# New entries in a list scheduler's table of times: changes of TensorE's form, scores, weighted values, early experts, and the delay of other engines' results

## The chip, the cores and the metric

One core of a Trainium2 chip runs the whole program. The metric is device time in microseconds of one execution; the kernel before takes 797.88 us (median of three runs). Its engines each work through a list of instructions of their own, in order: TensorE (matrix products and transposes; PE in the profile), VectorE (DVE), ScalarE (ACT), GpSimd (POOL), and SyncE (SP), which issues the transfers. Where one needs another's result it waits for it, and everything behind it on that engine waits too.

## The reference, cut to what matters

```python
scores = scale * np.matmul(q, k.transpose(0, 1, 3, 2))        # 2 batches, 8 heads, 576 x 576
x = (psi_rel / psi_i)[..., None]                              # from log distances of positions
bias = np.maximum(x @ w1 + b1, 0.0) @ w2                      # a network of 32 hidden units, for 8 heads
scores = scores + bias.transpose(2, 0, 1)[None, :, :, :]
attn = softmax(scores); x = np.matmul(attn, v)                # 1152 tokens x 512
for e in range(4):                                            # four experts, dense
    out += p[:, e:e + 1] * (np.maximum(x @ moe_w1[e], 0.0) @ moe_w2[e])
h = out @ w_in; g = h * np.cos(h); return g @ w_out           # 512 -> 2048 -> 512
```

## The kernel before, in words

The program is written as a graph of some 3750 steps. Each step names its engine, how long it is thought to take, what it reads and writes, and a function that emits its instructions. `Graph.order` plays the graph through on a clock of its own and so decides in which order every engine gets its instructions, which buffer a tile takes, and, for steps that two or three engines can do (`alts`), which engine does them. A step becomes ready when its inputs are done by that clock (plus `LAG` of the engine that made them) and a buffer is free; of the ready ones the one that was written down first is taken. The built program then has these orders fixed; the clock is not in it. So a number in the table of times changes no instruction, but may change every order.

TensorE runs in three forms: column tiles for the bias networks (L507, mode "columns"), row tiles for the scores (L700, mode "rows"), and the whole array for the rest. The table adds `SWITCH` to a step that changes the form.

The stages, by TensorE's work:
- The bias networks, 36 steps of 16 rows each (L507). Each needs masks that VectorE makes (L482) and ScalarE (L484, L486), and leaves two or three banks that VectorE combines (L515, L522) before SyncE writes them to memory.
- The first set of attention, the first 64 rows of all heads, in plain fp32: scores L667, transposes L652, values L676. It yields the first 128 tokens (`x0`).
- Early experts (`fill`): 7 halves of experts on these 128 tokens alone, first layer L1028 and second layer L1036 in fp32. They are written down after all else of attention and go wherever TensorE has nothing better.
- The second set, 512 rows of each head, in pairs of heads with every fp32 operand split into a high and a low fp32r half. One scoring product (`qk`, L700, 12 matmuls) serves two heads and 128 rows; then VectorE takes the row's extreme (L622), ScalarE the exponential (L625), VectorE the reciprocal in two small steps (L629, L631), GpSimd, VectorE or ScalarE scale (L635), TensorE transposes (L652), ScalarE and VectorE split into halves (L558, L560; tails L711, L713), TensorE makes the values (L720, 18 matmuls for a pair), ScalarE and VectorE add their halves (L723, L725). There are 32 scoring products. Two banks of scores exist, both taken by one product.
- The experts on all tokens (`run_ff`, `block_products`; first layer L773 and L913, second L782), their first layers split by L978 and L979, the weighted sums by L990 (the first for a tile) and L993. Weights are split by ScalarE or GpSimd (L548, L547) and VectorE or GpSimd (L549); L732 is the low half of a finished block of tokens.
- The last two layers with the cosine, on the same lines.

## Time and profile before

| what | us |
|---|---|
| median of three runs (795.89 to 800.22) | 797.88 |
| the profiled execution | 794.95 |
| its span, first to last instruction | 793.1 |
| TensorE busy in it | 776.9 |
| VectorE busy in it | 675.4 |
| ScalarE busy in it | 451.7 |
| GpSimd busy in it | 161.8 |

The granted clock of TensorE is 1.0 over the whole span. Busy time counts an instruction from its start to its modelled end, and successive instructions overlap a little; so for what a group costs I read from its start to the start of what follows it. A row of the timeline gives start, busy time, engine, line, what is written from what, and how many instructions; a bracket says how long the engine was idle before it and who released it. A matmul in plain fp32 stands as two records. Rows with "p1x" or "fx" are buffers that take over the place of earlier ones.

### The profile page before, as it was taken

How to read it: one execution, taken by the hardware profiler on the slowest of the kernel's cores; microseconds unless marked ns; L12 is line 12 of the kernel's file. 1: busy time of each engine (PE TensorE's matmuls, PEld its weight loads, DVE VectorE, ACT ScalarE, POOL GpSimd, SP SyncE). 2: the span in 40 equal slices, each digit the busy share in tenths (PEclk: the TensorE clock that was granted, in tenths of full speed). 3: DMA queues.
4: the chain of work that ended last, by engine and by line, in shares of the span. 5: the costliest groups of instructions: out<-in, count | busy, mean ns of one | idle time of the engine just before them, and what ended most of it. 6: DMA issues, size and time to landing. Idle time of an engine off the chain costs nothing.

```text
span 793.1 us, 15013 instructions
## 1 busy us (share of the span) xinstructions
PE 776.9 (98%) x5122; PEld 645.4 (81%) x5122; DVE 675.4 (85%) x1581; ACT 451.7 (57%) x956; POOL 161.8 (20%) x212
## 2 busy tenths in 40 slices
PE   7899999999999999999999999999999999999998
PEld 5575667888788878888888888888889889998997
DVE  8969998888889899578997989798879939999575
ACT  6667647787987752344563636272535637665352
POOL 0110055767985820135000000000000000000000
PEclk9999999999999999999999999999999999999999
DMA  6978989988755421645554453543453296769012
GB/s 216 293 257 254 287 305 285 274 265 249 234 161 172 133 81 41 194 163 185 176 199 147 133 199 119 193 152 125 129 184 107 91 337 208 248 218 305 25 43 79
DMA packets 98988, 148.08 MB, mean 187 GB/s; under 512 B 13280, under 2 KB 46688, under 8 KB 98912
## 3 DMA queue, kind: packets, MB, share of 16 engines
q1 hardware_dynamic: 98912, 147.13, 57.6%
q8 instruction: 40, 0.66, 0.3%
q14 instruction: 36, 0.29, 0.1%
HBM read 110.68 MB, written 36.41 MB: 185 GB/s over the span
## 4 chain that ended last, share of the span: by engine, by line
PE 89%; DVE 5%; DMA 2%; issue 1%; ACT 1%; SPq 1%; POOL 0%; DVEq 0%; ACTq 0%
PE p1x L782 20%; PE p L782 15%; PE p1x L913 10%; PE p1x L773 9%; PE p L913 7%; PE p L773 5%; PE p L507 4%; PE p L652 3%; PE p L1036 3%; PE p L720 3%; PE p L700 3%; PE p L1028 3%; PE p L676 1%; DVE bs L482 1%; DVE es L522 1%
## 5 line engine op out<-in xcount | busy, mean ns | idle before, releaser
L782 PE MATMUL p1x<-wx,hs 128*128 128x512 f32 (+1 forms) x708 | 166.7, 389 | 1.7 <-DVE hs L979 1.7
L782 PEld LDWEIGHTS p1x<-wx,hs 128*128 128x128 f32 x708 | 131.5, 188 | 28.9 <-DVE hs L979 2.3
L782 PE MATMUL p<-wx,hs 128*128 128x512 f32 (+1 forms) x516 | 122.9, 389 | 0.1
L782 PEld LDWEIGHTS p<-wx,hs 128*128 128x128 f32 x516 | 95.4, 188 | 19.7 <-DVE hs L560 0.3
L635 POOL TENSOR_SCALAR es<-es,stats 128x576 f32<-128x576 f32 (+2 forms) x104 | 63.1, 622 | 82.8 <-ACT bs L486 30.1
L773 PE MATMUL p1x<-xh,wx 128*128 128x384 f32 (+2 forms) x248 | 69.9, 355 | 0.0
L625 ACT ACTIVATE es<-es,stats 128x576 f32<-128x576 f32 x72 | 55.4, 771 | 15.4 <-DVE stats L622 5.7
L507 PE MATMUL p<-bs,wpc 128*32 128x288 bf16 (+3 forms) x1152 | 53.4, 321 | 5.9 <-DVE es L522 3.1
L622 DVE CUSTOM_DVE_ANT_0 es<-p,es 128x576 f32<-128x576 f32 x72 | 53.0, 751 | 4.5 <-PE p L700 2.1
L548 ACT ACTIVATE wx<-fs 128x512 fp32r<-128x512 f32 (+1 forms) x80 | 45.0, 582 | 19.8 <-DMA fs<-in_mw 10.0
L507 PEld LDWEIGHTS <-wpc 128*32 128x32 bf16 x1152 | 30.4, 96 | 27.5 <-issue 16.8
L773 PE MATMUL p<-xh,wx 128*128 128x384 f32 (+2 forms) x168 | 48.4, 353 | 0.6 <-DVE stats L629 0.6
L773 PEld LDWEIGHTS p1x<-xh,wx 128*128 128x128 f32 x248 | 45.4, 188 | 4.2
L482 DVE TENSOR_SCALAR bs<-cst,cneg 128x576 bf16<-128x576 f32 (+3 forms) x108 | 46.8, 472 | 0.0
L913 PE MATMUL p1x<-xh,wx 128*128 128x512 f32 (+1 forms) x144 | 45.8, 366 | 0.0
L560 DVE TENSOR_TENSOR hs<-p,hs 128x512 fp32r<-128x512 f32 x61 | 41.0, 685 | 3.4 <-ACT hs L558 2.7
L773 PE MATMUL p1x<-xl,wx 128*128 128x384 f32 (+2 forms) x124 | 43.9, 354 | 0.0
L549 POOL TENSOR_TENSOR wx<-fs,wx 128x512 fp32r<-128x512 f32 (+1 forms) x38 | 41.7, 1120 | 2.5 <-ACT wx L548 2.1
L652 PE MATMUL p<-ident,es 128*128 128x128 f32 x276 | 41.9, 278 | 0.3 <-POOL es L635 0.3
L913 PE MATMUL p1x<-tx,wx 128*128 128x512 f32 (+1 forms) x180 | 41.6, 367 | 0.0
L558 ACT ACTIVATE hs<-p 128x512 fp32r<-128x512 f32 x61 | 35.7, 594 | 9.4 <-PE p L652 8.8
L549 DVE TENSOR_TENSOR wx<-fs,wx 128x512 fp32r<-128x512 f32 (+1 forms) x56 | 36.7, 675 | 5.0 <-ACT wx L548 4.9
(237 smaller groups left out, 1686.8 us busy)
## 6 DMA issues: line engine op xcount, KB each, us to landing
fs<-in_mw SPq DMA_DIRECT2D x119, 256.0 KB, 4.1
wx<-winhl SPq DMA_DIRECT2D x32, 256.0 KB, 5.5
wx<-wouthl SPq DMA_DIRECT2D x32, 256.0 KB, 5.2
es<-biasD SPq DMA_DIRECT2D x24, 288.0 KB, 4.6
winhl<-fs SPq DMA_DIRECT2D x23, 256.0 KB, 2.8
wouthl<-fs SPq DMA_DIRECT2D x23, 256.0 KB, 3.2
fs<-in_win SPq DMA_DIRECT2D x22, 256.0 KB, 3.6
fs<-in_wout SPq DMA_DIRECT2D x20, 256.0 KB, 3.8
```

The lines of the kernel that those rows point to most:

```text
L482: e.tensor_scalar(out=mask(t), in0=tab[:, w0:w0 + W], scalar1=cneg[:, u:u + 1], scalar2=None, op0=ALU.is_ge)
L507: nc.tensor.matmul(out=pv(a)[32 * t:32 * t + 32], lhsT=wpc[:, i, 32 * kk:32 * kk + 32], rhs=mask(t, m * a, m), start=(i == 0), stop=(i == ...
L548: act = ("ACT", t_act(n, 0, 1), lambda: nc.scalar.activation(out=hv(), in_=fv(), func=AF.Copy))
L549: low = lambda e: e.tensor_tensor(out=lv(), in0=fv(), in1=hv().bitcast(F32), op=ALU.subtract)
L560: G.step("DVE", t_dve(n), lambda: nc.vector.tensor_tensor(out=dst(AL), in0=src(), in1=dst(AH).bitcast(F32), op=ALU.subtract), rd=[ps_, (AH ...
L622: G.step("DVE", t_dve(S) + 10, lambda: nc.vector.tensor_tensor_reduce(out=f3(bt.tile[:, :S]), in0=sp.tile[:, :, 0:288], in1=f3(bt.tile[:, ...
L625: exp_all.append(G.step("ACT", t_act(S, 1, 1) + 67, lambda: nc.scalar.activation(out=e.tile[:, :S], in_=bt.tile[:, :S], func=AF.Exp, scale ...
L635: nrm = lambda g: g.tensor_scalar(out=dst(), in0=src(), scalar1=rs, scalar2=1.0, op0=ALU.mult, op1=ALU.mult)
L652: nc.tensor.transpose(tp.tile[:, 128 * kt:128 * kt + 128], e.tile[:, 128 * kt:128 * kt + 128], ident)
L773: nc.tensor.matmul(out=z.tile[:, 0:n], lhsT=w[dt][2][wi]()[:, 128 * ft:128 * ft + 128], rhs=x[:, dt, p0:p0 + n], start=(dt == 0 and i == 0 ...
L782: nc.tensor.matmul(out=y.tile[:, 0:m], lhsT=hx, rhs=w[ft][2][wi]()[:, c0:c0 + m], start=(ft == 0 and i == 0), stop=(ft == nf - 1 and i == 2))
L913: nc.tensor.matmul(out=z.tile[:, 0:n], lhsT=x()[:, 128 * t:128 * t + 128], rhs=y(), start=(start and d == 0 and i == 0), stop=(d == 1 and ...
```

## The change

The table gets new numbers: what a change of form costs, per form, less the time that TensorE has been idle; how late results of other engines reach TensorE (`TO_PE`, used in place of `LAG` where the reader is TensorE); and the durations of the scoring product, the exponential, the two small steps, the values and the early experts' first layer. No step is added or taken away. The two lines that come in shift later line numbers by one or two.

```diff
-    SWITCH, STAY = 91.0, 0
+    TO_PE = {"ACT": 250.0, "DVE": 245.0, "POOL": 175.0, "DMA": 207.0}
+    SWITCH, STAY = {"columns": 93.0, "rows": 196.0, "": 196.0}, 0
...
-                    s.dur, mode = s.dur + self.SWITCH, s.mode
+                    s.dur, mode = s.dur + max(0.0, self.SWITCH[s.mode] - (now - eng_free[e])), s.mode
...
+                tp = s.end + s.lat + self.TO_PE.get(e, 0.0)
...
-                    k.rdy = max(k.rdy, s.end if same else t)
+                    k.rdy = max(k.rdy, s.end if same else tp if k.eng == "PE" else t)
...
-T_QK = 800.0
+T_QK = 770.0
...
-        exp_all.append(G.step("ACT", t_act(S, 1, 1) + 67, lambda: nc.scalar.activation(
+        exp_all.append(G.step("ACT", t_act(S, 1, 1) + 104, lambda: nc.scalar.activation(
...
-        G.step("DVE", 73, lambda: nc.vector.tensor_scalar(
+        G.step("DVE", 86, lambda: nc.vector.tensor_scalar(
...
-        G.step("DVE", 73, lambda: nc.vector.reciprocal(
+        G.step("DVE", 80, lambda: nc.vector.reciprocal(
...
-                G.step("PE", 9 * t_mm(256), av, rd=[V, AH, AL, AT], wr=[(bank, "av")])
+                G.step("PE", 9 * t_mm(256) + 33, av, rd=[V, AH, AL, AT], wr=[(bank, "av")])
...
-            ends["l1"] = G.step("PE", 4 * 218, l1, rd=w1s + [fix("x0")], wr=[z])
+            ends["l1"] = G.step("PE", 4 * 223, l1, rd=w1s + [fix("x0")], wr=[z])
```

It changes the orders from the first microseconds on. Three places follow; `p` are banks of PSUM, `es` the tiles of scores and bias, `bs` the masks.

First place, VectorE in the first set of attention. Before, the seventh and the eighth pass over scores (L622) and what stands between:

```order
L622 ISA es_135,stats<-p_162,es_135 128x576
L622 ISA stats 128x1
L684 COPY x_82<-p_157 64x64
L629 TENSOR_SCALAR stats<-stats 128x1
L631 RECIPROCAL stats<-stats 128x1
L565 COPY es_134<-p_156 64x128
L622 ISA es_133,stats<-p_162,es_133 128x576
```

And now, around the sixth and the seventh pass (L624):

```order
L517 SCALAR_TENSOR_TENSOR es_134<-p_154,cst 128x512
L484 TENSOR_SCALAR bs_152<-cst,cneg 128x384
L524 SCALAR_TENSOR_TENSOR es_134<-p_157,es_134 128x512
L624 ISA es_138,stats<-p_162,es_138 128x576
L624 ISA stats 128x1
L484 TENSOR_SCALAR bs_149<-cst,cneg 128x384 x3
L460 RECIPROCAL psum_p<-psum_p 128x9
L517 SCALAR_TENSOR_TENSOR es_138<-p_154,cst 128x384
L631 TENSOR_SCALAR stats<-stats 128x1
L624 ISA es_132,stats<-p_161,es_132 128x576
```

Pieces of the bias (L517 and L524, which were L515 and L522, and the masks L484, which were L482) now stand between the passes over scores, where before only the pieces of the first set stood.

Second place, VectorE at the beginning of the second set, around the first two passes over scores. Before:

```order
L522 SCALAR_TENSOR_TENSOR es_138<-p_157,es_138 128x288
L622 ISA es_133,stats<-p_162,es_133 128x576
L622 ISA stats 128x1
L622 ISA es_134,stats<-p_161,es_134 128x576
L622 ISA stats 128x1
L522 SCALAR_TENSOR_TENSOR es_139<-p_156,es_139 128x288
L629 TENSOR_SCALAR stats<-stats 128x1
L522 SCALAR_TENSOR_TENSOR es_139<-p_155,es_139 128x288
```

Now:

```order
L524 SCALAR_TENSOR_TENSOR es_142<-p_154,es_142 128x288
L624 ISA es_139,stats<-p_162,es_139 128x576
L624 ISA stats 128x1
L624 ISA es_131,stats<-p_161,es_131 128x576
L624 ISA stats 128x1
L551 TENSOR_TENSOR ks_128<-fs_104,ks_127 128x512
L631 TENSOR_SCALAR stats<-stats 128x1
L624 ISA es_140,stats<-p_161,es_140 128x576
```

The last bias pieces now all stand ahead of the first pass; on TensorE the first two scoring products, which had 24 bias matmuls (L507) between them, now stand one behind the other.

Third place, TensorE at the hand-over to the experts, right behind the last value product. Before, the end of a second-layer group (L782) and the first-layer group behind it (L773):

```order
L782 MATMUL p_157<-wx_3194,hs_94 128x512
L782 MATMUL p_157<-wx_3195,hs_94 128x512
L773 MATMUL p1x_4020<-xh,wx_3091 128x512
L773 MATMUL p1x_4020<-xl,wx_3091 128x512
L773 MATMUL p1x_4020<-xh,wx_3091 128x512
L773 MATMUL p1x_4020<-xh,wx_3070 128x512
```

Now:

```order
L784 MATMUL p_155<-wx_3325,hs_89 128x512
L784 MATMUL p_155<-wx_3324,hs_89 128x512
L775 MATMUL p_155<-xh,wx_3904 128x384
L775 MATMUL p_155<-xl,wx_3904 128x384
L775 MATMUL p_155<-xh,wx_3905 128x384
L775 MATMUL p_155<-xh,wx_3264 128x384
```

Before, the first-layer group wrote another bank than the group ahead of it; now it writes the same one, p_155. Between the scoring products themselves there are now far fewer expert products (L775, L784) and more early ones (L1030, L1038).

## Rows read from the trace of the kernel before

**Rows 1.** The page's first part: busy us, share of the span, instructions.
```profile
PE 776.9 (98%) x5122; PEld 645.4 (81%) x5122; DVE 675.4 (85%) x1581; ACT 451.7 (57%) x956; POOL 161.8 (20%) x212
```

**Rows 2.** Busy us of each engine in five stretches (start:end, length, engines, clock, DMA).
```profile
core 0: us, PE busy (x) PEld busy (x) DVE busy (x) ACT busy (x) POOL busy (x), PEclk, DMA share, GB/s
...
40.00:60.00 20.00, 20.00 (x201) 14.52 (x193) 13.59 (x42) 12.56 (x32) 2.98 (x4) 1.00 0.80 261
...
100.00:115.00 15.00, 14.31 (x272) 9.39 (x270) 14.06 (x30) 5.66 (x11) 7.58 (x8) 1.00 0.84 285
115.00:263.00 148.00, 144.82 (x1132) 120.65 (x1132) 128.68 (x380) 119.34 (x278) 110.08 (x156) 1.00 0.75 229
263.00:300.00 37.00, 35.22 (x198) 30.88 (x198) 34.42 (x61) 21.96 (x47) 16.39 (x19) 1.00 0.39 114
...
500.00:550.00 50.00, 50.00 (x223) 41.40 (x222) 44.78 (x100) 22.32 (x47) 0.00 (x0) 1.00 0.45 146
```

**Rows 3.** TensorE's waits: line, for whom, us in total, times, longest.
```profile
PE p L507 <- DVE es L522: 3.1, 3, 1.7
PE p L720 <- DVE ht L713: 2.1, 2, 1.8
PE p1x L782 <- DVE hs L979: 1.7, 1, 1.7
```

**Rows 4.** Timeline of TensorE around the first two scoring products.
```profile
112.34 1.06 PE L700 MATMUL p<-ks,ks 64*128 64x288 f32 x12
113.33 0.92 PE L507 MATMUL p<-bs,wpc 128*32 128x288 bf16 x24
114.94 1.06 PE L700 MATMUL p<-ks,ks 64*128 64x288 f32 x12 [0.69 <-DVE stats L622]
```

**Rows 5.** VectorE in the first set (timeline), and the last bias pieces (groups by shape).
```profile
45.97 0.22 DVE L684 COPY x<-p 64x64 f32<-64x64 f32 x1 [0.54 <-PE p L676]
...
L522 DVE SCALAR_TENSOR_TENSOR es<-p,es 128x288 f32<-128x288 f32 x16 | 6.8, 449 | 0.1
```

**Rows 6.** Timeline of TensorE in the bias stage, with early experts.
```profile
62.76 2.94 PE L1028 MATMUL p<-x,fs 128*128 128x128 f32 x24
65.63 2.29 PE L507 MATMUL p<-bs,wpc 128*32 128x384 bf16 x48
...
70.38 1.98 PE L1036 MATMUL p<-fs,fs 128*128 128x512 f32 x4
72.29 2.46 PE L507 MATMUL p<-bs,wpc 128*32 128x448 bf16 x48
```

**Rows 7.** The chain that ended last, in order of time: start, us, what.
```profile
329.81 10.88 PE p1x L782 x48
```

**Rows 8.** VectorE's groups by shape: busy us, mean ns of one, idle before.
```profile
L622 DVE CUSTOM_DVE_ANT_0 es<-p,es 128x576 f32<-128x576 f32 x72 | 53.0, 751 | 4.5 <-PE p L700 2.1 <-PE p L667 1.7
L560 DVE TENSOR_TENSOR hs<-p,hs 128x512 fp32r<-128x512 f32 x61 | 41.0, 685 | 3.4 <-ACT hs L558 2.7
L713 DVE TENSOR_TENSOR ht<-p,ht 64x256 fp32r<-64x256 f32 x30 | 12.7, 422 | 0.5
L631 DVE RECIPROCAL stats<-stats 128x1 f32<-128x1 f32 x72 | 11.2, 159 | 1.3
```

**Rows 9.** Timeline at the hand-over: VectorE, then GpSimd.
```profile
281.56 2.39 DVE L549 TENSOR_TENSOR wx<-fs,wx 128x512 fp32r<-128x512 f32 x2
283.88 1.77 DVE L732 TENSOR_TENSOR xl<-fx,xh 128x512 fp32r<-128x512 f32 x1
...
286.16 1.28 DVE L549 TENSOR_TENSOR wx<-fs,wx 128x512 fp32r<-128x512 f32 x2
...
280.99 1.81 POOL L549 TENSOR_TENSOR wx<-fs,wx 128x512 fp32r<-128x512 f32 x1 [0.78 <-ACT wx L548]
283.56 1.53 POOL L549 TENSOR_TENSOR wx<-fs,wx 128x512 fp32r<-128x512 f32 x1 [0.76 <-ACT wx L548]
```

**Rows 10.** VectorE's first weighted sum of an expert's tile, by shape.
```profile
L990 DVE TENSOR_SCALAR fs<-p1x,prob 128x512 f32<-128x512 f32 x2 | 1.5, 752 | 2.2 <-PE p1x L782 1.4 <-issue 0.8
```

More of the change, by code (lines that the diff above doesn't have):

```diff
@@ L624, in unit @@
             op0=ALU.add, op1=ALU.min, accum_out=stats[:, 0, c:c + 1]), rd=[sp, bt], wr=[bt, (st, "m")])
-        exp_all.append(G.step("ACT", t_act(S, 1, 1) + 67, lambda: nc.scalar.activation(
+        exp_all.append(G.step("ACT", t_act(S, 1, 1) + 104, lambda: nc.scalar.activation(
             out=e.tile[:, :S], in_=bt.tile[:, :S], func=AF.Exp, scale=-1.0, bias=stats[:, 0, c:c + 1],
             accum_out=stats[:, 1, c:c + 1]), rd=[bt, (st, "m")], wr=[e, (st, "s")], after=trn_all[-AHEAD:1 - AHEAD]))
-        G.step("DVE", 73, lambda: nc.vector.tensor_scalar(
+        G.step("DVE", 86, lambda: nc.vector.tensor_scalar(
             out=stats[:, 2, c:c + 1], in0=stats[:, 1, c:c + 1], scalar1=1e-9, scalar2=None, op0=ALU.add), rd=[(st, "s")], wr=[(st, "t")])
-        G.step("DVE", 73, lambda: nc.vector.reciprocal(out=stats[:, 3, c:c + 1], in_=stats[:, 2, c:c + 1]), rd=[(st, "t")], wr=[(st, "r")])
+        G.step("DVE", 80, lambda: nc.vector.reciprocal(out=stats[:, 3, c:c + 1], in_=stats[:, 2, c:c + 1]), rd=[(st, "t")], wr=[(st, "r")])
         rs = stats[:, 3, c:c + 1]
```

## Prediction, made before the changed kernel ran

> **What bounds the kernel now.** I began with the page's first part: TensorE is busy for 776.9 us of the span of 793.1 [rows 1]. So an order of instructions can give back at most the 16.2 us in which TensorE stood idle, and some of that lies before the first operand has landed and after the last product, where no order reaches it. Then I cut the span into stages [rows 2]. From 300 us on nothing is to be had: TensorE is busy for all of 500 to 550, and the same products are left to do. The idle time sits in three places: the start (the bias networks), the scoring stage from 115 to 263 us, where TensorE works 144.82 of 148 us and so loses 3.2, and the hand-over to the experts from 263 to 300, where it loses 1.8. The waits name the releasers, and they are all on VectorE [rows 3]: 3.1 us in three waits of the bias products for L522, 2.1 in two waits of the value products (L720) for the low half of a probability tile (L713), 1.7 in one wait at the hand-over. VectorE is therefore the second thing to watch: the change has to serve it better, or it does nothing.
>
> **What the change removes.** No arithmetic goes or comes. In the order of TensorE I count 105 changes between its three forms (column tiles for the bias, row tiles for the scores, whole array) before and 103 after. A change costs some 0.2 us by the scoring products: twelve of them take 0.99 us from their start to the next start, against 0.77 that the table now holds for them [rows 4]. Two fewer, and one more folded into a wait: **-0.3 us**.
>
> **The start, up to the second scoring product.** TensorE's order is the same for the first 32 us. In the first set of heads the trace has VectorE idle for 6.4 of the 20 us from 40 to 60 [rows 2]; it waits for products of early scores and of early values, again and again for about half a microsecond, as in the first of [rows 5]. The new order puts bias pieces there (first place shown above). In exchange it takes 16 early-expert products of the first kind and 4 of the second out of the bias stage and puts them among the scores. Their price: twelve of the first kind take 2.87 us up to the next start, so 0.22 each after about 0.2 for the form; two of the second kind take 1.91, so 0.86 each [rows 6]. That is 16 x 0.22 + 4 x 0.86 = 7.0 us of TensorE work that comes later, and not less work. With the form change saved, TensorE would reach its second scoring product 7.3 us sooner than the 114.94 us of [rows 4], at 107.6. Can VectorE follow? Before that product TensorE needs the first two passes over scores (L622). In the old order two of the last bias pieces (L522) stand behind these passes, in the new order none does (second place): 2 x 0.449 [rows 5], so 0.9 us more VectorE work in front of them. Filling the whole hole of 6.4 and doing 0.9 more leads to 114.94 - 6.4 + 0.9 = 109.4 us; filling it and also the idle 0.9 of 100 to 115 [rows 2] leads to 108.5. TensorE arrives 0.9 to 1.8 us before it is let go. The two scoring products also stand back to back now, without the 24 bias products that filled 0.9 us between them [rows 4]; the wait for L622, 0.69 there, grows by as much, but this is the same wait, since TensorE was early anyway. So this stretch costs **+1.3 us**, between -1.0 (TensorE's own idle of 0.7 between 100 and 115 goes as well) and +4.0 (only half of the hole is filled).
>
> **The scoring stage.** The new order takes 90 expert products (L773, L782) out of it and puts the 7.0 us above in. At 0.227 us each (48 of them in 10.88 us, [rows 7]) that is 20.4 - 7.0 = 13.4 us less TensorE work, done later without loss, for those products fill TensorE wherever they stand. What changes the span is only the idle time. Two waits for L713 make up 2.1 of the 3.2 us [rows 3]. The new table lets results of VectorE reach TensorE 245 ns after their end instead of 165, counts the form changes at 196 instead of 91, and so no longer places a value product where it arrives a little early. I take 2.1 us back, **-2.1**. Bounds: -3.2 if all the idle time goes, and as much the other way, +3.2, because VectorE becomes tighter. Per scoring product it has two passes L622 (751 ns), two L560 (685), L713 and L725 (422, the same width) and four small ones (159): 4.35 us by [rows 8], some 4.0 where one starts before the other has ended. 31 of them are 124 us, without the splits and the early experts' sums. The stage shrinks from 148 to about 148 - 13.4 - 2.1 = 132.5. VectorE is busy for 128.68 us of it now, 87% [rows 2], the experts' work included, and would be at about 94%.
>
> **The hand-over.** The wait of 1.7 us goes: it came because two splits took 2.39 us and the low half of the last block (L732) 1.77, where the two splits right after it took 1.28 [rows 9]; GpSimd was running its own splits at 280.99 and 283.56. In the new order L732 is never on VectorE. A new wait takes its place: the last value product is followed by two second-layer groups, and the first-layer product after them writes the bank that the second of these has just filled (third place). The bank must be scaled out first by L990, 0.75 us [rows 10], and the two signals around it add, by the table, about 0.5. What is queued behind it are TensorE's own 60 first-layer products, and nothing else that is ready. 1.2 - 1.7 = **-0.5 us**, between -1.7 (another engine's delay lets the bank be free) and +1.5 (L990 itself is late by a slow split).
>
> **The rest** is TensorE without a gap before and after; moved pieces of the weight conversion have more than enough time there. 0, within 0.5.
>
> Sum: -0.3 + 1.3 - 2.1 - 0.5 = -1.6 us on the profiled execution: span 791.5, its time 794.95 - 1.6 = 793.35. The median of the three runs shown, 797.88, lies 2.9 above the profiled run; the timed kernel is compared with that, so I predict 797.88 - 1.6 = 796.3 us.
>
> **Rivals.** *VectorE becomes the bound of the scoring stage (slower).* For it: 94% by the sum above, and a VectorE instruction that meets a GpSimd one is stretched: 2.39 against 1.28 us for two splits, and 1.77 for L732, in [rows 9]. The new order gives VectorE 9 more splits of 512 columns, 3 of them among the scores. It decides from the point where VectorE's 8.5 us of slack in the stage are gone. Each stretched instruction costs about 0.55 us, so 15 of them use it up; with 24 stretched ones TensorE waits 5 us: 797.88 - 1.6 + 2.1 + 5 = 803.4. Against it: the stage had GpSimd busy for most of it already, and TensorE lost only 3.2 us.
> The Trainium skill (SBUF — State Buffer, Who interferes with whom) says that a VectorE instruction with two SBUF inputs contends with a GpSimd instruction that reads SBUF, and that the loser blocks for the whole instruction. The trace agrees that they contend [rows 9], but the delay there is 0.55 us an instruction where GpSimd's take 1.5 or more. By a full block of 1.5 us, 15 stretched instructions would cost 22.5 - 8.5 = 14 us, which gives 812; by the trace's 0.55 they use up the slack and cost nothing yet.
> *VectorE and TensorE fit together (clearly faster).* The hole is filled without the 1.3 us, all 3.2 us of the scoring stage go, and the hand-over loses nothing: -0.3 - 1.0 - 3.2 - 1.7 = -6.2, which is 791.7. For it: the waits in [rows 3] are short ones, of the size of the corrected delays. Against it: five separate gaps would all have to close.
> *The table changes nothing that is felt.* The new order stalls as often in other places: 797.9. It is within my forecast's own range.
>
> **How the numbers follow.** 0.5%, about what a measurement of this kernel can tell from no change, is 4 us. Forecast with the no-effect case, 793.9 to 801.9: 0.60. Clearly faster, about 791.7: 0.25. VectorE as the bound, about 803.4: 0.15. The range from 791.7 to 801.5 leaves out most of the slow rival and the tail beyond the fast one.
>
> **What would show it.** Right: the second scoring product starts at 108 to 110 us; VectorE is busy for over 17 of 20 us from 40 to 60; the last scoring product starts between 238 and 243 us instead of 263; no wait for L732's neighbours but one of about 1.2 us for L990 right after the last value product; TensorE without idle time from 300 on. Wrong: a second scoring product after 112 us, waits of TensorE for L713, L622 or L560 of over 5 us in sum, splits of over 1 us on VectorE by the dozen, or a gap beyond 300 us.

## The result: 0.67% slower, and the profile after

The kernel after takes 803.33 us, the median of ten runs; the kernel before 797.72 beside it (ten runs, 795.24 to 800.78). One of the ten runs of after took 4402.44 us and is left out of the ratio, which is 1.0067, with a 95% interval from 1.0045 to 1.0089; the nine others lie between 801.92 and 806.36 and have a median of 802.95, so the loss is some 5.3 us. I had forecast 796.3, in a range from 791.7 to 801.5. So the time moved the other way, and out of the range. The span of the profiled execution is 800.7 us, 7.6 more than before. That is 2.3 us more than the loss by the medians: the profiled execution of before, 794.95 us, was faster than each of its ten runs.

The page of the kernel after, its first line (answers to [rows 1]) and the line of the chain that ended last, shares of the span by engine:

```profile
PE 780.4 (97%) x5122; PEld 645.0 (81%) x5122; DVE 682.4 (85%) x1594; ACT 446.2 (56%) x943; POOL 162.8 (20%) x212
...
PE 76%; DVE 13%; DMA 4%; issue 3%; ACT 2%; POOL 1%; SPq 0%; DVEq 0%; POOLq 0%; ACTq 0%
```

TensorE shows 3.5 us more of busy time for the same products. Successive products overlap in the trace (one of 512 columns stands with 0.39 us at 270.18, and the next starts 0.23 us behind it, at 270.41), so a delay shorter than the overlap shows as busy time. So the loss of 7.6 us is larger than the added idle time, and the windows alone don't show it. They are those of [rows 2], cut where this kernel's stages end (the last scoring product starts at 243.57 us):

```profile
core 0: us, PE busy (x) PEld busy (x) DVE busy (x) ACT busy (x) POOL busy (x), PEclk, DMA share, GB/s
40.00:60.00 20.00, 20.00 (x202) 14.09 (x201) 18.10 (x54) 13.74 (x35) 3.99 (x7) 1.00 0.92 294
100.00:115.00 15.00, 12.80 (x185) 8.92 (x184) 13.40 (x35) 6.11 (x15) 10.59 (x12) 1.00 0.95 314
115.00:243.00 128.00, 124.90 (x1019) 102.71 (x1019) 117.13 (x351) 103.39 (x243) 91.68 (x135) 1.00 0.82 251
243.00:300.00 57.00, 53.38 (x288) 45.09 (x287) 55.56 (x106) 31.20 (x70) 32.85 (x31) 1.00 0.35 111
300.00:400.00 100.00, 99.44 (x456) 82.33 (x456) 77.94 (x174) 41.99 (x87) 16.78 (x14) 1.00 0.53 177
```

The hole of VectorE from 40 to 60 us is filled, as forecast. From 243 to 300 us VectorE is busy for 55.56 of 57 us, and TensorE loses 3.6 us there that can be seen. Its waits (compare [rows 3]; line, for whom, us in total, times, longest):

```profile
PE p L509 <- DVE es L517: 3.0, 6, 0.6
PE p L702 <- DVE stats L624: 2.5, 3, 1.5
PE p L509 <- DVE bs L484: 2.0, 3, 1.1
PE p L775 <- DVE hs L981: 1.7, 2, 1.2
...
PE p L784 <- DVE fs L995: 1.0, 1, 1.0
PE p L722 <- DVE ht L715: 0.9, 3, 0.4
PE p L775 <- DVE fs L992: 0.9, 1, 0.9
...
PE p1x L775 <- DVE fs L1197: 0.5, 1, 0.5
```

The waits of 2.1 us for L713 (now L715) shrank to 0.9. The one of 1.7 for L979 (now L981) became two of 1.7 together. L992, L995 and L1197 are new, and the scoring products' waits for a pass over scores (L624, before L622) grew from 1.0 to 2.5.

To place the whole 7.6 us I added up, along TensorE's order, what its products take back to back in the trace, and subtracted that from the time at which a product starts. The difference is the time lost up to there, seen or hidden:

| time lost by TensorE (us) up to | before | after | grown by |
|---|---|---|---|
| the second scoring product | 14.4 | 17.0 | 2.6 |
| the last scoring product | 18.4 | 21.2 | 2.8 |
| 300 us | 20.7 | 26.9 | 6.2 |
| the end | 22.3 | 30.1 | 7.8 |

So the start costs 2.6 us, the scoring stage 0.2, the hand-over (from the last scoring product to 300 us) 3.4, and what comes after it 1.6. The forecast for the four was +1.3, -2.1, -0.5 and 0.

How good are these four? Counted again, with the median step from one product to the next for each kind, they are 2.3, 0.2, 3.2 and 1.9. From one execution to another the start is the uncertain one: three profiles with before's order up to there (before, and short_splits_before and scale_on_act_before of the experiments) have the second scoring product at 114.94, 116.04 and 116.79 us, so up to 1.9 us of the 2.6 may lie in which execution of before was profiled. The hand-over is steady: by this second count it loses 2.2, 2.0 and 2.2 us in those three, and 5.4, 5.2 and 5.6 in after, short_splits_after and scale_on_act_after.

### What TensorE waits for in the hand-over

The timeline of the kernel after, TensorE from the end of the attention on (start, us, engine, line, what; in brackets the idle time before and its releaser):

```profile
261.81 2.95 PE L784 MATMUL p<-wx,hs 128*128 128x512 f32 x12
265.66 0.45 PE L775 MATMUL p<-xh,wx 128*128 128x384 f32 x1 [0.90 <-DVE fs L992]
...
271.98 0.50 PE L775 MATMUL p<-xh,wx 128*128 128x512 f32 x1 [1.18 <-DVE hs L981]
...
282.98 3.02 PE L784 MATMUL p<-wx,hs 128*128 128x512 f32 x12 [1.04 <-DVE fs L995]
```

And the banks that these groups write, by TensorE's order:

```
second layer,  6 products  p_156
second layer,  6 products  p_155
first layer,  12 products  p_155   265.66, waits for L992 to read p_155
first layer,  12 products  p_156
first layer,  12 products  p_155   271.98, waits for L981 to read p_155
first layer,  12 products  p_156
first layer,  12 products  p_154
second layer,  6 products  p_156
second layer,  6 products  p_155
second layer,  6 products  p_156   282.98, waits for L995 to read p_156
```

Two banks by turns: a group finds its bank still full of what TensorE put there in the group just before (265.66) or one group earlier, 1.4 to 2.7 us ago. Why VectorE has not emptied it shows in VectorE's own timeline, with the first half of the emptying on ScalarE (L980) below:

```profile
264.85 0.75 DVE L992 TENSOR_SCALAR fs<-p,prob 128x512 f32<-128x512 f32 x1
265.52 4.73 DVE L551 TENSOR_TENSOR wx<-fs,wx 128x512 fp32r<-128x512 f32 x6
...
271.38 0.55 DVE L981 SCALAR_TENSOR_TENSOR hs<-p,hs 128x384 fp32r<-128x384 f32 x1
...
268.07 0.49 ACT L980 ACTIVATE hs<-p 128x384 fp32r<-128x384 f32 x1 [0.20 <-PE p L775]
```

ScalarE is done with the bank at 268.56. The half of it that VectorE does takes 0.55 us, but starts at 271.38, behind six splits of weights (4.73 us) and two sums. One of the six, from 268.46, takes 1.78 us instead of 0.68, beside a split on GpSimd (VectorE's two last splits as shortest/median/longest in ns, then GpSimd's):

```profile
L551 DVE TENSOR_TENSOR wx<-fs,wx x2: 679/1232/1784, 267.9 to 268.5; 128x512 fp32r<-128x512 f32 x2
...
267.95 1.75 POOL L551 TENSOR_TENSOR wx<-fs,wx 128x512 fp32r<-128x512 f32 x1 [2.10 <-ACT wx L550]
```

This left two readings. Either VectorE has too much to do (theory A below), or the planner gives out the wrong bank: it takes the buffer that came free last (the list of free buffers is used from its end), so any delay of the emptying falls on TensorE, while other banks have been free for longer (theory E).

### The profile page after: what moved, and what is told of

It reads as the page before. It is cut to its first block, busy times and chain, and to the rows that moved or that the text cites. A ratio compares the mean times of both kernels' runs of the same rounds, so it can differ in the third digit from the quotient of the medians.

```text
span 800.7 us, 14982 instructions
## 1 busy us (share of the span) xinstructions
PE 780.4 (97%) x5122; PEld 645.0 (81%) x5122; DVE 682.4 (85%) x1594; ACT 446.2 (56%) x943; POOL 162.8 (20%) x212
## 4 chain that ended last, share of the span: by engine, by line
PE 76%; DVE 13%; DMA 4%; issue 3%; ACT 2%; POOL 1%; SPq 0%; DVEq 0%; POOLq 0%; ACTq 0%
PE p L784 23%; PE p L915 11%; PE p L775 9%; PE p1x L784 8%; PE p1x L915 5%; PE p L722 3%; PE p L509 3%; PE p L702 3%; PE p L654 2%; PE p1x L775 2%; PE p L1030 2%; DVE es L624 2%; DVE bs L484 2%; PE p L1038 2%; PE p L678 1%
## 5 line engine op out<-in xcount | busy, mean ns | idle before, releaser
L784 PE MATMUL p<-wx,hs 128*128 128x512 f32 (+1 forms) x912 | 212.9, 388 | 1.0 <-DVE fs L995 1.0
L784 PEld LDWEIGHTS p<-wx,hs 128*128 128x128 f32 x912 | 168.5, 188 | 35.9 <-DVE fs L995 1.5
L775 PE MATMUL p<-xh,wx 128*128 128x512 f32 (+2 forms) x344 | 97.4, 356 | 2.6 <-DVE hs L981 1.7
L784 PE MATMUL p1x<-wx,hs 128*128 128x512 f32 x312 | 74.3, 390 | 0.0
L775 PEld LDWEIGHTS p<-xh,wx 128*128 128x128 f32 x344 | 62.8, 188 | 10.6 <-DVE hs L981 2.9
L784 PEld LDWEIGHTS p1x<-wx,hs 128*128 128x128 f32 x312 | 58.4, 188 | 12.1
L775 PE MATMUL p<-xl,wx 128*128 128x512 f32 (+2 forms) x172 | 61.0, 354 | 0.0
L624 DVE CUSTOM_DVE_ANT_0 es<-p,es 128x576 f32<-128x576 f32 x72 | 53.3, 751 | 3.5 <-DMA es<-biasD 1.5
L915 PE MATMUL p<-xh,wx 128*128 128x512 f32 (+1 forms) x172 | 55.7, 371 | 0.0
L509 PEld LDWEIGHTS <-wpc 128*32 128x32 bf16 x1152 | 30.5, 96 | 28.4 <-issue 18.4
L551 DVE TENSOR_TENSOR wx<-fs,wx 128x512 fp32r<-128x512 f32 (+1 forms) x69 | 44.1, 662 | 6.3 <-ACT wx L550 6.2
L980 ACT ACTIVATE hs<-p 128x512 fp32r<-128x512 f32 (+2 forms) x50 | 28.6, 572 | 36.8 <-PE p L775 22.7
L484 DVE TENSOR_SCALAR bs<-cst,cneg 128x576 bf16<-128x576 f32 (+3 forms) x108 | 46.6, 467 | 0.0
L562 DVE TENSOR_TENSOR hs<-p,hs 128x512 fp32r<-128x512 f32 x62 | 41.8, 686 | 2.5 <-ACT hs L560 1.9
L915 PE MATMUL p<-tx,wx 128*128 128x512 f32 (+1 forms) x186 | 43.8, 371 | 0.0
L995 DVE SCALAR_TENSOR_TENSOR fs<-p,prob,fs 128x512 f32<-128x512 f32 x42 | 31.3, 744 | 12.7 <-PE p L784 12.7
```

The costliest lines, as they stand in the source:

```text
L484: e.tensor_scalar(out=mask(t), in0=tab[:, w0:w0 + W], scalar1=cneg[:, u:u + 1], scalar2=None, op0=ALU.is_ge)
L509: nc.tensor.matmul(out=pv(a)[32 * t:32 * t + 32], lhsT=wpc[:, i, 32 * kk:32 * kk + 32], rhs=mask(t, m * a, m), start=(i == 0), stop=(i == ...
L551: low = lambda e: e.tensor_tensor(out=lv(), in0=fv(), in1=hv().bitcast(F32), op=ALU.subtract)
L562: G.step("DVE", t_dve(n), lambda: nc.vector.tensor_tensor(out=dst(AL), in0=src(), in1=dst(AH).bitcast(F32), op=ALU.subtract), rd=[ps_, (AH ...
L624: G.step("DVE", t_dve(S) + 10, lambda: nc.vector.tensor_tensor_reduce(out=f3(bt.tile[:, :S]), in0=sp.tile[:, :, 0:288], in1=f3(bt.tile[:, ...
L775: nc.tensor.matmul(out=z.tile[:, 0:n], lhsT=w[dt][2][wi]()[:, 128 * ft:128 * ft + 128], rhs=x[:, dt, p0:p0 + n], start=(dt == 0 and i == 0 ...
```

## Experiments

The time beside each ratio is the median of that kernel; ratios are to the kernel before on the same chip, with a 95% interval.

One thing has to be known for differences of 2 us and less. In part of the executions, before and after the change, TensorE's granted clock stands at half (0.5, so 1.2 instead of 2.4 GHz) for 3.41 or 6.83 us; in the profiles that have it, it begins between 109 and 139 us. The mean over the span is then 0.993 to 0.998. Here is the same stretch without it, in the kernel before, and with it, in short_splits_before (0.79 over 8 us), and eight products of the same pair of heads in each:

```profile
136.00:144.00 8.00, 7.88 (x73) 7.28 (x74) 6.39 (x21) 6.46 (x16) 6.68 (x11) 1.00 0.89 287
...
136.00:144.00 8.00, 6.78 (x48) 6.42 (x49) 5.65 (x18) 5.05 (x13) 5.15 (x8) 0.79 0.87 278
...
137.26 1.12 PE L720 MATMUL p<-hs,ks 128*128 128x256 f32 x8
...
138.63 1.91 PE L721 MATMUL p<-hs,ks 128*128 128x256 f32 x8
```

TensorE had waited 1.83 us for L713 (L714 there) just before, in both; so that wait alone does not decide it. Of 35 runs of before on one chip, the 20 with a mean of 0.998 or less have a median of 798.8 us, the 15 others 796.5. How many of a kernel's runs have it differs: none of 12 of only_switch, all 12 of only_to_pe, 10 of 12 of only_durations.

### One part of the change at a time

`only_switch`, `only_to_pe` and `only_durations` put into the kernel before one part of the diff each; `all_but_to_pe` takes one part out of the kernel after:

```diff
-                    k.rdy = max(k.rdy, s.end if same else tp if k.eng == "PE" else t)
+                    k.rdy = max(k.rdy, s.end if same else t)
```

> The kernel before with one part of the change alone: a change of TensorE's form counts 93 or 196 ns, less any idle time ahead of it, instead of 91. By the durations in the trace of before, its order puts 243.6 us of TensorE work ahead of the last scoring product (before 244.6, after 222.3). Theory A (VectorE sets the end up to 300 us; whoever pulls the scoring stage forward leaves the experts' splits and sums for VectorE to do in a bunch at the hand-over, and pays 0.25 us for each us pulled forward): 798 us, like before. Theory B (the delays towards TensorE are the harmful part): 798. Theory C (any new order moves the time by some us, whatever the numbers mean): anywhere from 794 to 804.

> The kernel before with the delays of other engines' results towards TensorE alone (245 to 250 ns instead of 160 to 165 from VectorE and ScalarE). 239.6 us of TensorE work stand ahead of the last scoring product. Theory A: 799 (5 us pulled forward, 1.2 us paid). Theory B: 802 to 804, most of the loss of 5.6 us. Theory C: 794 to 804.

> The kernel before with the steps' durations alone (exponentials, the two small statistics, weighted values, early first-layer products). 241.7 us of TensorE work stand ahead of the last scoring product. Theory A: 798.5. Theory B: 798. Theory C: 794 to 804.

> The kernel after without the delays towards TensorE; all other corrections stay. 229.7 us of TensorE work stand ahead of the last scoring product, two thirds of the way from before to after. Theory A: 801.5 (15 us pulled forward, 3.7 us paid). Theory B: 798. Theory C: 794 to 804.

| kernel | us | ratio | TensorE work ahead of the last scoring product, us |
|---|---|---|---|
| only_switch | 797.25 | 0.9991 (0.9976 to 1.0006) | 243.6 |
| only_to_pe | 799.82 | 1.0016 (0.9998 to 1.0033) | 239.6 |
| only_durations | 800.26 | 1.0024 (1.0004 to 1.0043) | 241.7 |
| all_but_to_pe | 801.94 | 1.0045 (1.0028 to 1.0062) | 229.7 |
| after (nine runs) | 802.95 | 1.0067 (1.0045 to 1.0089) | 222.3 |

No single part holds the loss, so theory B (the delays towards TensorE do the harm) falls: without them 0.45 of the 0.67% are still there. The orders that pull the scoring stage forward most take longest, as theory A said; only_durations is 1.8 us above it. The three single parts themselves can't be told apart: with runs of like granted clock, only_to_pe and only_durations are 0.8 and 1.8 us over before (means), and only_switch 0.2.

### Less work for VectorE

First a move: the same order, the first weighted sums issued on ScalarE.

```diff
-            G.step("DVE", t_dve(512, 1), lambda: nc.vector.tensor_scalar(
-                out=a(), in0=y.tile, scalar1=pc, scalar2=None, op0=ALU.mult), rd=[y, fix("pw")], wr=[acc[t]])
+            G.step("DVE", t_dve(512, 1), lambda: nc.scalar.activation(
+                out=a(), in_=y.tile, func=AF.Copy, scale=pc), rd=[y, fix("pw")], wr=[acc[t]])
```

> The kernel after, every engine's order kept, but the first weighted sum of each block of tokens (L992 there, nine instructions of 0.75 us) is issued on ScalarE instead of VectorE. Four of the nine stand on VectorE between 262 and 265.6 us of the profiled run, ahead of six splits (4.7 us) and of the step L981 for which TensorE then waits. Theory A (VectorE is late as a whole in the hand-over, its queue is a bunch of experts' splits and sums): VectorE is 3 us earlier there, so the waits of TensorE for L992 (0.9), L981 (1.2) and L995 (1.0) go or shrink: 803.3 - 3 = 800.3. Theory D (each of these waits has its own cause: the banks' order, an early product's place): only the wait for L992 goes, 802.4.

> The same on the kernel before, where TensorE has one wait of 1.7 us in the hand-over (for L979), made by two slow splits beside GpSimd. Theory A: VectorE has little in the hand-over to be late with, gain 0 to 1.7: 797. Theory D: 797.7, no change.

Measured: 804.8 us on after (1.0093, 1.0069 to 1.0116) and 798.4 on before (1.0017, 1.0003 to 1.0032). It gained on neither, though VectorE was busy for 2.8 us less from 243 to 300 us on after, and 1.8 less on before. (Four of the six runs on after have a granted clock of 0.993 to 0.998; so it can't be said that it became slower.) TensorE's waits from 243 us on:

```profile
PE p L775 <- ACT fs L992: 2.8, 1, 2.8
PE p L784 <- DVE fs L995: 1.0, 1, 1.0
...
PE p L775 <- DVE hs L981: 0.2, 1, 0.2
```

The wait for L981 nearly went, as theory A had it. Both theories had the wait for L992 go too. That wait became three times as long instead, because the four L992 now stand in ScalarE's list between its own splits (ScalarE first, then the product of TensorE that the last of them lets go):

```profile
267.75 0.69 ACT L992 ACTIVATE fs<-p,prob 128x512 f32<-128x512 f32 x1
268.33 1.45 ACT L550 ACTIVATE wx<-fs 128x256 fp32r<-128x256 f32 x3
...
271.34 0.94 ACT L550 ACTIVATE wx<-fs 128x256 fp32r<-128x256 f32 x2
272.17 0.69 ACT L992 ACTIVATE fs<-p,prob 128x512 f32<-128x512 f32 x1
...
272.91 0.44 PE L775 MATMUL p<-xh,wx 128*128 128x384 f32 x1 [2.76 <-ACT fs L992]
```

Whoever empties the bank, TensorE waits for that engine's place in line. (The profiled execution also lost 4 us more than after by its second scoring product, in waits for a split on GpSimd (1.8) and for a load (1.5), so the whole of its time cannot be put down to L992.)

Then a cut: less work for VectorE in the scoring stage. Planned were 22 us; the trace shows 12.7 us less of busy time there.

```diff
+        cut = (lambda x: x[:, 0:1]) if n_units[0] >= 24 else (lambda x: x)
...
-            out=dst(AL), in0=src(), in1=dst(AH).bitcast(F32), op=ALU.subtract), rd=[ps_, (AH, key)], wr=[(AL, key)], off=O_EVC)
+            out=cut(dst(AL)), in0=cut(src()), in1=cut(dst(AH).bitcast(F32)), op=ALU.subtract), rd=[ps_, (AH, key)], wr=[(AL, key)], off=O_EVC)
```

> The kernel after, order kept. From the 25th block of rows on, the split of the transposed probabilities on VectorE (L562, 512 columns, 0.68 us) writes a quarter of its columns: the low parts of the other columns are left out. 48 instructions, some 0.45 us each, 22 us less for VectorE between 130 and 260 us. Theory A: the loss in the scoring stage (4.2 us) shrinks to about 1.5, and VectorE comes to the hand-over early, so its 5 us shrink to about 2: 803.3 - 6 = 797.3. Theory D: the scoring stage gains its 2.7, the hand-over does not change: 800.6. If neither moves, VectorE is not what TensorE waits for: 803.

> The same on the kernel before. Theory A: scoring stage from 4.0 us lost to 1.5, hand-over from 2.3 to 1.5: 797.7 - 3.3 = 794.4, so a gain about half of that of the kernel after. Theory D: 797.7 - 2.5 = 795.2, the same gain as on the kernel after.

Measured: 802.25 us on after (1.0066, 1.0048 to 1.0085) and 795.99 on before (0.9971, 0.9957 to 0.9984). On after that is no gain at all by the ratio, where theory A had 6 us. Two windows of short_splits_after, and TensorE's waits from 243 us on (this kernel's lines stand one higher):

```profile
115.00:243.00 128.00, 124.97 (x1028) 103.26 (x1029) 104.42 (x355) 103.81 (x244) 93.38 (x137) 1.00 0.82 252
243.00:300.00 57.00, 53.37 (x293) 45.37 (x291) 53.09 (x107) 32.00 (x73) 32.71 (x31) 1.00 0.35 112
```

```profile
PE p L776 <- DVE hs L982: 1.8, 2, 1.2
PE p L785 <- DVE fs L996: 1.0, 1, 1.0
PE p L776 <- DVE fs L993: 0.9, 1, 0.9
```

VectorE falls from 117.13 to 104.42 us in the stage, and TensorE is busy for 124.97 us instead of 124.90. The time lost between the second and the last scoring product is 4.3 us (4.2 in the kernel after). So VectorE's load does not set the scoring stage of the kernel after. On before the cut did gain, 2.1 us by the medians and clear of 1 by the ratio, near theory D's 2.5. Its profile seems to deny it (4.3 us lost in the stage instead of 4.0), but it has the clock at half for 3.41 us just there, in the rows above: from the first of those value products to the next scoring product it takes 3.46 us instead of 2.31, and that scoring product 1.33 instead of 1.00. Without these 1.5 us the stage loses 2.8. So on before VectorE's load seems to have cost about 1.2 us there, by this estimate; why it costs nothing on after is open. In the hand-over of after the three waits are the same to 0.1 us, with VectorE busy for 53.09 of the 57 us: it does the experts' work no earlier. (That its operands come no earlier is what I infer; no run tried it.) Theory A falls on after, and D's gain of 2.7 us in the scoring stage came on before only.

### Another bank

One word in the planner changes which of the free buffers is handed out. The engines' orders and all durations stay; only the names of the buffers differ.

```diff
-                        b.slot = b.tile = free[b.cls].pop()
+                        b.slot = b.tile = free[b.cls].pop(0 if b.cls == "P1" else -1)
```

For `oldest_all` it is `pop(0)` in every class; for `second_bank_after` the last but one in class P1.

> The kernel after, every engine's order kept, but the planner hands out of the free PSUM banks of 512 columns the one that has been free longest, instead of the one freed last. In the hand-over of the kernel after, groups of twelve products go to two banks by turns, so a group waits for ScalarE and VectorE to empty the bank that TensorE filled one group (2.7 us) earlier; by the order, 187 of 272 groups come back to a bank within three groups, here 63. Theory E (what TensorE waits for from 244 us on is such a bank, never an operand): the waits for L992 (0.9), L981 (1.2 and 0.6), L995 (1.0) and L1197 (0.5) go, some 4.5 us: 803.3 - 4.5 = 798.8. Theory A (VectorE is late as a whole in the hand-over, whichever bank is taken): the operands come late instead, 803.

> The same on the kernel before. Its one wait of the hand-over (1.7 us for L979, 2.3 with what it hides) goes by theory E: 797.7 - 2.0 = 795.7. By theory A 797.7. If E holds for both, what is left between after and before is 3 us, that of the start and the scoring stage.

> The kernel after with the buffer that has been free longest in all classes, those in SBUF too. Theory E: like the banks alone, 798.8, within 1; or up to 2 us below it where a load waited for a buffer freed just before (TensorE's waits for the bias tiles and for the keys' load in the start). Theory A: 803.

> The same on the kernel before. Theory E: 795.7, or up to 2 us below it. Theory A: 797.7.

> The kernel after, order kept, the bank freed last but one handed out instead of the one freed last: a half dose. By the order 31 groups come back to a bank after one group between (52 in the kernel after, 24 with the oldest bank), 79 after two (133 and 33). Theory E: between the two, 803.3 and 798.4, at about 800. Theory H (the gain came from something else in the oldest-bank order, the banks p1x or the start, and not from the distance): 803 or 798, at one of the ends.

| kernel | us | ratio | new sums begun in a bank with at most one group between, of 210 | with exactly two between |
|---|---|---|---|---|
| after (nine runs) | 802.95 | 1.0067 (1.0045 to 1.0089) | 105 | 14 |
| second_bank_after | 800.16 | 1.0027 (1.0014 to 1.0040) | 10 | 93 |
| oldest_bank_after | 798.35 | 1.0016 (1.0004 to 1.0027) | 0 | 0 |
| oldest_all_after | 796.99 | 0.9997 (0.9987 to 1.0007) | 0 | 0 |
| before, beside them | 797.40 | 1 | 101 | 14 |
| oldest_bank_before | 795.60 | 0.9970 (0.9958 to 0.9982) | 0 | 0 |
| oldest_all_before | 794.59 | 0.9965 (0.9951 to 0.9978) | 0 | 0 |

The counts are by the order of the built programs, over all of TensorE's groups, and take only experts' groups that begin a new sum, 210 in each kernel: only such a group needs its bank emptied. (The 272 of the expectations take in groups that go on adding to a sum in a bank, which needs no emptying; so the numbers there are others.) The habit is as common in before as in after. The five runs came within 0.5 us of the first number of theory E, but for oldest_all (1.8 and 1.1 us lower, inside what it allowed). The half dose, in effect three banks by turns, lies between the ends, so theory H falls as well. TensorE's waits from 243 us on, and the window of the hand-over, for oldest_bank_after:

```profile
PE p1x L654 <- DVE stats L624: 0.7, 1, 0.7
PE p1x L784 <- DVE hs L981: 0.7, 1, 0.7
```

```profile
243.00:300.00 57.00, 55.63 (x306) 47.91 (x306) 55.98 (x113) 33.26 (x76) 29.95 (x32) 1.00 0.38 121
300.00:400.00 100.00, 100.00 (x461) 83.53 (x460) 80.07 (x180) 43.74 (x91) 16.80 (x14) 1.00 0.53 179
```

VectorE is as full as in after (55.98 of 57 us), and yet TensorE gains 2.25 us in the window and has no gap from 300 to 400. The six splits are as slow as in after, and no wait for L981 follows them. The one that is left in the list comes at 295.32, inside a group of six, so it is for an operand (the first row is VectorE's, the others TensorE's):

```profile
267.94 4.79 DVE L551 TENSOR_TENSOR wx<-fs,wx 128x512 fp32r<-128x512 f32 x6
...
293.32 1.33 PE L784 MATMUL p1x<-wx,hs 128*128 128x512 f32 x5
295.32 1.88 PE L784 MATMUL p1x<-wx,hs 128*128 128x512 f32 x7 [0.68 <-DVE hs L981]
```

So it was the bank, and not VectorE's load alone: a full VectorE is late with each evacuation, and this hurts where the next group needs that very bank. By the second count above, from the last scoring product to the end after loses 8.2 us, oldest_bank_after 2.9, before 3.1 and oldest_bank_before 1.3. In the kernel before, with VectorE busy for 51.27 us from 243 to 300, the same habit cost one wait of 1.7 us:

```profile
243.00:300.00 57.00, 55.13 (x347) 47.71 (x346) 51.27 (x112) 36.73 (x80) 31.93 (x42) 1.00 0.42 124
```

With the oldest bank that one is gone too: oldest_bank_before has no wait of TensorE after 243 us in its list.

So with the oldest banks after is 0.16% over the kernel before instead of 0.67. But before gains by them too, 0.30%: like with like, 0.46% stay between the two, 2.75 us, close to the 3 that the expectation left to the start and the scoring stage.

The Trainium skill (Perfetto Trace Analysis, Matmuls) says that independent matmul groups should rotate through different PSUM banks, so that the evacuation of one overlaps the products of the next. The runs agree, and add how far: two banks by turns already count as different ones, and cost 0.51% here, 4 us, against taking all of them in turn.

### Is the rest in the start?

With the oldest buffers after is still 0.32% slower than before (0.9997 against 0.9965, 2.4 us). For the start, the masks were cut:

```diff
+                X = W // 2 if s >= 16 else 0
-                e.tensor_scalar(out=mask(t), in0=tab[:, w0:w0 + W], scalar1=cneg[:, u:u + 1], scalar2=None, op0=ALU.is_ge)
+                e.tensor_scalar(out=mask(t, X, W - X), in0=tab[:, w0 + X:w0 + W], scalar1=cneg[:, u:u + 1], scalar2=None, op0=ALU.is_ge)
```

> The kernel after with the longest-free buffer in all classes (797.0), order kept; from bias step 16 on VectorE's masks (L484) write the upper half of their columns only (the rest is left out): 0.12 to 0.15 us less each, some 7 us between 40 and 108 us. Theory F (what is left of the loss is the start: VectorE works without a gap from 40 to 108 us and sets when the second scoring product starts, 109.3 us): that product comes at 107 to 107.6 us, and the time falls by 2 to 3 us to 794.5. Theory G (the start of both kernels waits for VectorE alike): as much as on the kernel before.

> The same on the kernel before with the longest-free buffer (794.6). VectorE has 6 us of idle time from 40 to 60 us there. Theory F: 0.5 to 1 us, 794; the two kernels are then within 1 us. Theory G: 2 to 3 us, 792; the 2.4 us between them stay.

Measured: 796.03 us (0.9985, 0.9971 to 1.0000) and 794.56 (0.9965, 0.9950 to 0.9979): 1.0 us and nothing, with intervals that overlap. VectorE from 40 to 100 us, first in oldest_all_after, then in short_masks_after:

```profile
40.00:100.00 60.00, 58.89 (x851) 39.45 (x852) 56.44 (x136) 39.47 (x81) 6.89 (x13) 1.00 0.81 258
...
40.00:100.00 60.00, 59.40 (x853) 39.60 (x854) 50.75 (x138) 39.24 (x81) 6.79 (x13) 1.00 0.81 259
```

It has 5.7 us less to do, and the second scoring product starts at 108.97 us instead of 109.34. So its load is not what holds that product, and theory F is not borne out; nor is G, by which both kernels would have gained 2 to 3 us. Where the last 2.4 us are stays open.

### The same with other orders

> The kernel after without the delays towards TensorE, and with the longest-free buffer in all classes. Without the latter it took 801.9, 1.4 less than after. Theory E: it falls by the same 5 to 6 us as after did, 796.5; what the single corrections are worth is then below what these runs tell apart. Theory B (the delays towards TensorE did harm of their own): 795 or less, at least 1.5 below the kernel after with the same buffers (797.0).

> The kernel before with the changes of form counted anew (as in only_switch, 0.9 per mille under before there) and with the longest-free buffer in all classes (794.6 on the kernel before). Theory E: the two add up, 794 (793 to 795). Theory C (any new order moves the time by some us): 792 to 798.

> The kernel before with the steps' durations alone (800.3 with the buffer freed last, 1.9 over before) and with the longest-free buffer in all classes. Theory E: the buffers take away what a late evacuation costs, whatever the order: 800.3 - 4 = 796. Its order makes 11 form changes more than before, 1.7 us of TensorE work, so not under 795. Theory C: 792 to 800.

| order | buffer freed last | buffer free longest |
|---|---|---|
| before | 1 | 0.9965 (0.9951 to 0.9978) |
| only the changes of form | 0.9991 | 0.9968 (0.9956 to 0.9979) |
| only the durations | 1.0024 | 0.9966 (0.9950 to 0.9981) |
| all but the delays | 1.0045 | 0.9985 (0.9971 to 1.0000) |
| after | 1.0067 | 0.9997 (0.9987 to 1.0007) |

The spread over five orders falls from 0.76% to 0.32%. Three of them are now alike, though two of these hold 11 or 12 more changes of form than before, some 1.7 us of TensorE work. That does not make the changes free: four of the six runs of oldest_all_before have a granted clock of 0.997 or 0.998 (mean 795.2 us) and two the full one (793.8), while all 24 of the two others have 0.999 or 1.0 (795.5 and 795.4). With like clock the two are some 1.6 us slower, though two runs are few. So much of what theory C calls the luck of the order was the buffers. What is left still rises with how far the scoring stage is pulled forward. The best kernel of all is the one before with the longest-free buffers, 794.59 us: 0.35% better than before, 1.0% under after.

## Why the prediction was wrong, point by point

**The step that failed first is the hand-over (-0.5, measured +3.4).** The mechanism was named: a first-layer group that writes the bank just filled, and waits for VectorE. I had found it at one place of the order, priced it once at 1.2 us (0.90 seen there at 265.66), and took the old wait off. The same happens again two groups later (1.18) and at 282.98 (1.04), and it is the rule and not an accident: 105 of 210 new sums have at most one group between. But it is the rule in before too (101), which paid one wait of 1.7 us for it. What the sum had wrong is the price. It is not the length of L992, but what stands ahead of the evacuation in VectorE's list, and the new order fills that list: VectorE is busy for 55.56 of 57 us there, before for 51.27. Handing out the oldest bank, with VectorE just as full, brought the time from 0.67% over before to 0.16%.

**The rest (0, measured +1.6).** I argued that TensorE has no gap from 300 us on, from [rows 2], where this is so for the order of before. It was no law of the stage. One window, 500 to 550, had stood for all of it. Two waits of 0.56 and 0.55 us (for L981 at 352.36 and for L1197 at 685.58) came in; they are not in the list of oldest_bank_after, so they were for a bank.

**The scoring stage (-2.1, measured +0.2).** I let the two waits for L713 go, and they did shrink, from 2.1 to 0.9 us. Waits for the split L562 (0.6) and for GpSimd (0.2) came in, those for a pass over scores are 1.0 as before, and of the 4.2 us lost there these waits show 2.7. The step that failed: a planner that knows delays better places one product better, but the order is new everywhere, and I priced only what the old one lost. The last scoring product starts at 243.57, a little after the 238 to 243 of the forecast.

**The start (+1.3, measured +2.6, with the doubt told above)** lies within its bounds, -1.0 to +4.0. VectorE's hole was filled (18.10 of 20 us; I had asked for over 17). The second scoring product came at 110.23 us, just outside the 108 to 110:

```profile
107.26 1.43 PE L702 MATMUL p<-ks,ks 64*128 64x288 f32 x12
110.23 1.05 PE L702 MATMUL p<-ks,ks 64*128 64x288 f32 x12 [1.54 <-DVE stats L624]
```

The wait between the two has grown from 0.69 [rows 4] to 1.54, as the text had said, for nothing stands between them any more; there is also one of 1.11 us for masks (L484) at 85.37.

**The changes of form (-0.3)** are too small to be seen. By their own price, 0.99 - 0.77, two fewer and one folded in are 0.4 to 0.7 us. Whether eleven more of them cost the 1.7 us of that price, oldest_all_durations leaves open: nothing by the medians, some 1.6 us with like clock.

**The rivals.** The slow one gave 803.4 us, and 803.3 was measured, but that is luck. It put the loss into the scoring stage, by VectorE's load (94% there) and by 24 of its instructions stretched beside GpSimd; VectorE is at 92% there (117.13 of 128 us), short_splits_after shows that 12.7 us less do not help, and in the whole of each kernel only three of VectorE's splits (L551, L562, L715, and before the change also L732) take over 1 us. Their price was misread as well. The 2.39 us for two splits in [rows 9] are one of 1.79 and one as short as ever:

```profile
L549 DVE TENSOR_TENSOR wx<-fs,wx x4: 674/678/1786, 281.6 to 286.8; 128x512 fp32r<-128x512 f32 x4
```

So a stretched one costs 1.1 us and not 0.55, nearer to the full block that the prediction set aside: it ends 0.55 us after GpSimd's (281.56 to 283.35 beside 280.99 to 282.80). That price counts in the hand-over: of the lateness behind the wait of 1.18 us, 1.1 are the one stretched split. What I had not among the rivals is that buffers are part of the planner's order. Of my signs for "wrong" it was the last that came, a gap beyond 300 us.

## What to carry to other kernels

When a table of times is corrected and the kernel becomes slower, look first at what the planner leaves without slack: a buffer that is handed out again the moment it comes free turns a late evacuation into a wait. Hand out the one that has been free longest; here it made each of the five orders faster and took more than half of the spread between them away. And where the order shows one group that reuses a bank at once, count all of them, in both kernels, and price each by what stands ahead of the evacuation on its engine.

## What the runs showed that I had not expected

- Banks alone, with every list of instructions in the same order, are worth 0.51%, 4 us (oldest_bank_after), and 1.0% lies between the slowest and the fastest of the ten kernels in the last table, which do the same arithmetic.
- VectorE busy for 97 to 98% of a stretch (55.56 and 55.98 of 57 us) let TensorE lose 3.6 us with one choice of banks and 1.4 with another.
- A stretch of 3.41 us in which TensorE is granted half its clock comes in some executions and not in others, and is as large as the differences between the single parts of the change (2.3 us between the medians of before with and without it).
